# Attention rows replicated through one transpose and DRAM, loads spread over 16 blocks, later output stores, a tanh ring of ten, a new order of work

## The chip, the cores and the metric

The kernel runs on one core of a Trainium2 chip. The metric is the device time of one execution in microseconds. A profile is one further execution; its span is some 2 us shorter than the time taken for it. As there is one core, a run is called slow here only when it is more than 1.5% above the fastest of the same kernel. The kernel before was timed in every session beside what it is compared with; its medians in the five sessions were 735.8 to 738.6 us.

## The reference, cut to what matters

```python
B, N, m, C = (4, 12416, 32, 128)
def mab(q, kv):                         # attention of q over kv
    s = scale * (q @ kv.transpose(0, 2, 1)); s = s - s.max(-1, keepdims=True)
    a = np.exp(s); a /= a.sum(-1, keepdims=True) + 1e-09
    return a @ kv
h = mab(I, x)                           # 32 inducing rows attend to all 12416 tokens of a batch
x = mab(x, h)                           # every token attends to those 32 rows
gate = 1.0 / (1.0 + np.exp(-(x @ w_gate)))          # then a gated feed-forward layer, 128 -> 1536 -> 128
out = (gate * (x @ w_val)) @ w_out
```

The h of a batch needs all of its x. So the next batch is loaded, transposed and reduced to h while the present batch is in the feed-forward layer.

## The kernel before: the parts that matter

Tokens go through in 97 blocks of 512, 24 blocks a batch and one mixed block of tails. In each block PE makes gate and value columns (the fills, one helper line), ScalarE takes the tanh of the gates into a ring of T tiles, VectorE multiplies (1 + T) by the value out of PSUM, and PE multiplies by w_out. A string, PLAN, fixes the order of these within each block; the letter J in it takes the next of the extra jobs (scores, h, and so on) of the next batch. In 23 of the blocks ScalarE copies three of the twelve value columns to SBUF, and GpSimd multiplies them.

```python
tp = ctx.enter_context(tc.tile_pool(name="tp", bufs=8))          # the tanh ring
def load_x(b, q):            # 512 KB of fp16, cast on the way: issued by GpSimd
    nc.gpsimd.dma_start(t[:], x[b, ds(q * QT, QT)].rearrange("(p j) c -> p (j c)", j=QT // P))
def xT_dma(b, q):            # transposed for the scores: issued by SyncE
    nc.sync.dma_start(xTs[b][...], xqs[(b, q)][:], transpose=True)
# attention weights of 2048 tokens: normalize, repeat for four row groups, transpose 512 KB
for r in range(4):
    nc.gpsimd.tensor_tensor(out=a2[:, r], in0=e2n[...].to_broadcast(...), in1=rc[...].to_broadcast(...), op=ALU.mult)
nc.sync.dma_start(rep[:, 4 * i:4 * i + 4]..., a2[:]..., transpose=True)
# value columns that GpSimd takes; reads the tanh tile
nc.gpsimd.tensor_tensor(out=t[:], in0=v, in1=Ts[(bi, j0 // 2)][:, j0 % 2 + jj, :], op=ALU.mult)
nc.gpsimd.tensor_tensor(out=u[:, jj, :], in0=t[:], in1=v, op=ALU.add)
# ... cut: prologue, h, output; output transposes are issued by SyncE, output stores by GpSimd
```

The softmax here doesn't subtract the row's maximum and nothing guards it: scores larger than these inputs give would overflow.

Of the kernel before, what the change touches and what calls it, by code (L numbers as in the profile page):

```python
# [22 lines left out]


PLAN = (
    "GAGBWGAabGBcGAfeGBdGAhBWgJ AGilkjBGGAabcBGfAGBedWAGhBGg AGilBkjAGJBabAGcfBWeAGdBgGh "
    "AGilkBjGAGBabcGAefGBdGAhgBGi AGlBJkAGjBWAGBbacfGAedGBghG AikljBJGAaWBbcGAfeGBdGAhBGgG "
    "AilGBkjAGBWabGAceBGfGAdhgiBG AGlkBjJAGBbGacAGfeBGdG AgBJhAGilBkjGAGbaBceAGfdGBgG "
    "AhiGBlGAkjJBGAGbaBGcGAeBJf AGdhBGgAGiBlkjGAGBabef AGcdGBhGAgiBkljGAGBabceAGfBJdG "
    "AhgiBGAGlkjBJGABbWacfGAeBdGgh AGikGBlGAjJBGAGbacBfeGAGdhBgG AikGBlGAjJBGAGabBGcGAfeBGd "  # L30
    "AGhgiBGAGlkjBJGABaGbfG AeGcBdGAhgBWiJkljAGBGabcGAfedBgG AGhiBlGAJkBjAGGBabcGAfGBedG "
    "AhJBgGAikljBGGAabfBecG AGBdghGAilkjBGGAbaBcfGAGBedG AhGBgiGAlkjBGGAbacBGfAGBedGh "
    "AGgBiGAGklBjGAGBbacfAGedBGh AGgBGiAGkljBGGAabBcefGAGdhBgG AilkjBGGAbaBceGAGfdBhG "
    "AgGBikGAljBWGAabcBeGAGfdBhG AgGBikGAljBGGAbaGBcGAefGBdG AhBJgAGilkBjGAGbBaeG "
    "AfcGBdGAghBGiGAlkjBGAGbacBfG AeGBdhGAgiWBlGAkjBJGAbacBfeG AGdBghiGAlkjBJGAaGbBcGAfGeBdG "
    "AhGgBiGAlGkBjGAGBbacfAGedBGg AGhiBGlAGkjBJAGBGbaeG AfGcBdGAgJBhGAikljBGGAabcBfeG "
    "AdghBiGGAlkBjJAGBabcGGAfeBGdG AgBJhAGilkBjGAGaBbfe AGdcGBgGAhikBljGAGBabceAGfBJdG "
    "AhgBGiAGlkjBJGABbGaceGAfdWBhg AGiGBklGAjJBGAGbaBcWAGfeBdG AhGBgiGAlGBkGAjJBGAGbGBacG "
    "AfeGBdGAhgBGiGAlkjBJG AabGBfeAGdGBhgGAciBWlJkjAGBGbacG AfBJeAGdhGBgGAikljBGGAbBJa "
    "AGceBGfAGdBhGgAGiBlkjG AGBabefAGdgBGhcAGilkjBGGAabcBeG AfGdBhGAgGBilGAkjBWGAabBcGe "  # L40
    "AGfBGdAGgBhWAGiBlkjAGGBbace AGfdBGhAGgilBkjAGGBbacGAeGfBdG AhGBgiGAlkjBWGAabBefdG "
    "AGcBhgGAilkjBGGAabcBeGAfGdBhG AgGBiGAlkjBGGAbaBcGGAfeBdG AGhBGgAGilBkjAGJBba "
    "AGfeBGdAGcBhgGAGilkBjGAGBbace AGfBJdAGhgiBGAGkljBWAGBbacfeG AdGBhgGAikljBJGAaWBbcGAefGBdG "
    "AghGBiGAlBGkjAGBWbaAGcfBGe AGdgBhiGAGklBjJAGBGabf AGeBJdGAchBGgAGiklBjGAGaBbce "
    "AGfdGBgGAhiGBkGAljJBGAGbaBGcG AfBJeAGdgBGhAGilkBjG AGBabefAGdgBGhGAcikBljGAJbBac "
    "AGefBGdGAhgBiGAGlkjBJGABWbacfG AGeBdhgAGikGBlGAjJBGAGabBcefG AGdhBgGAilGBkGAjJBGAGabBGcG "
    "AfeBGdAGhgBGiAGlkjBJG ABabGfeAGdBhGgGAciBWlJkjAGBGabcG AeBJfAGdhGBgGAiklBjGGAbaBcfG "
    "AGeBdhgGAilkjBGAJeBfG AbWBadGAhgGBcGAilkjBGGAbacBfG AeGBdGAgGhBiGAlkjBGGAabBcGf "
    "AGedBGhAGgBiGAGlkBjGAGBbacf AGedBGhAGgBGiAGkljBGGAabcBefG AdgGBhGAilkjBGGAbaBfeG "
    "AdGBcgGAhGBilGAkjBWGAabcBfG AGedBgGAhGBilGAkjBGGAbBJa AGcfBGeAGdgBGhAGilkBjG "  # L50
    "AGBbafeAGdgGBhGAcikBljGAGBabce AGfdGBhGAgikBljGAGBbacfAGedgGBhG "
    "AikljBGGAabcBGAfWBedGAhgGBiG AlkjBJGAbGBacGAfeBGdGAhGBgiG AlkjBGGAbafBeGAdWBhgG "
    "AcGBilGAkjGBGAabBceGAfGdBG AhGgBiGAkljBGGAbaBcfGAGBJe AGdhBGgAGiklBjGAGBefba "
    "AGdhGBgGAickBljGAGBbaceAGfdBWgG AhikBljGAGBbacGAfeBGdGAhgiGBG AkljBGGAbacBGAfWBedGAhGBgiG "
    "AlkjBGGAbacBGAGfeBGAGdhBgiG AGkBljGAGBbafAGeBdgG AGhcBiGAGkBljGAGBabcAGfBeGd "
    "AGgBGhAGilBkjGAGBbacGAfGBedG AhgGBiGAlkBjGGAbBafeG AdGBchGAgGBilGAkjBWGAbacBefG "
    "AGBdghGAilBkjGGAbaBcfGAedGBhG AgiGBlGAkjBWGAabBceGAfGdBhG AgGiBkGAljBGGAbacBeGAGfdBhgiG "
    "AlkjBGGAabBefcGAdhBgGG AiklBjGABabcAfedBAghBilkj"
)
SHARED = (2, 7, 10, 15, 18, 23)  # L60


@with_exitstack
def kernel(
# [28 lines left out]
    ep = ctx.enter_context(tc.tile_pool(name="ep", bufs=2))  # L93
    ap_ = ctx.enter_context(tc.tile_pool(name="ap", bufs=2))
    repp = ctx.enter_context(tc.tile_pool(name="repp", bufs=2))
    tp = ctx.enter_context(tc.tile_pool(name="tp", bufs=8))
    up = ctx.enter_context(tc.tile_pool(name="up", bufs=5))
    vp = ctx.enter_context(tc.tile_pool(name="vp", bufs=1))
    outp = ctx.enter_context(tc.tile_pool(name="outp", bufs=3))
    smp = ctx.enter_context(tc.tile_pool(name="smp", bufs=2))  # L100

# [263 lines left out]

    def a2_mul(b, d, i):
        e2n, rc = e2s[(b, d)], e2s[(b, d, "rc")]
        a2 = ap_.tile([P, 4, 4, 4, M], F16, tag="a2", name=f"a2_{b}_{d}_{i}")
        for r in range(4):
            nc.gpsimd.tensor_tensor(  # L370
                out=a2[:, r], in0=e2n[:, i, :, r, :].unsqueeze(2).to_broadcast((P, 4, 4, M)),
                in1=rc[:, i, :, r].unsqueeze(2).unsqueeze(3).to_broadcast((P, 4, 4, M)),
                op=ALU.mult,
            )
        e2s[(b, d, i, "a2")] = a2

    def rep_tile(b, d):
# [1 line left out]
            reps[(b, d)] = repp.tile([P, 8, 4, P], F16, tag="rep", name=f"rep_{b}_{d}")  # L379
        return reps[(b, d)]  # L380

    def rep_dma(b, d, i):
        rep = rep_tile(b, d)
        a2 = e2s.pop((b, d, i, "a2"))
        nc.sync.dma_start(
            rep[:, 4 * i:4 * i + 4].rearrange("p r j t -> p (r j) t"),
            a2[:].rearrange("p r j g m -> p (r j g m)"), transpose=True,
        )


    blocks = []
# [276 lines left out]

    BB = 8 * ND
    ev = {}  # L670
    extra = {}

    def at(n, k, fn, *a):
        ev.setdefault((n, k), []).append(lambda: fn(*a))

    def put(n, *a):
        assert n not in extra
        extra[n] = a

    def rep_events(n, b, d):  # L680
        put(n, "s2", b, d)
        at(n + 1, 1, e2_dma, b, d)
        at(n + 1, 3, s2_sum, b, d)
        at(n + 2, 3, s2_rec, b, d)
        at(n + 2, 3, a2_mul, b, d, 0)
        at(n + 3, 1, rep_dma, b, d, 0)
        at(n + 3, 1, a2_mul, b, d, 1)
        at(n + 4, 0, rep_dma, b, d, 1)

    def m_mul():  # L690
        e2s["m", "a2"] = s2n_mul("m", 0, nc.gpsimd, B)
# [11 lines left out]
    def q1_dma(r):  # L703
        rep_blk(e2s["q1", r], 4 + r)

    put(0, "s2q")
    at(1, 0, s2n_sum, "q1", 0, 16)
    for r in range(4):
        at(1, r, q1_mul, r)
# [3 lines left out]
    for b in range(B):  # L713
        n0 = b * BB
        rep_events(n0 + 2, b, 1)
        rep_events(n0 + 10, b, 2)
        nb = b + 1
        if nb < B:
            plan = (
                ((1, 0), (2, 0), (2, 2), (3, 2), 4, (5, 2), (7, 9)),  # L720
                ((5, 0), (6, 0), (6, 2), (7, 2), 8, (9, 2), (12, 13)),
                ((8, 0), (9, 0), (9, 3), (10, 2), 11, (12, 2), (14, 15)),
            )
            for e, (l0, l1, x0, x1, s1, a1, hs) in enumerate(plan):
                qs = [2 * e, 2 * e + 1]
                for q, lo, xo, h in zip(qs, (l0, l1), (x0, x1), hs):
                    at(n0 + lo[0], lo[1], load_x, nb, q)
                    at(n0 + xo[0], xo[1], xT_dma, nb, q)
                    put(n0 + h, "h", nb, q)
                if e == 0:  # L730
                    at(n0 + l1[0], l1[1], load_tail, nb)
                    at(n0 + x1[0], x1[1], xTt_dma, nb)
                put(n0 + s1, "s1", nb, qs)
                at(n0 + a1[0], a1[1], a1_dma, nb, qs)
            put(n0 + 5, "s1t", nb)
            put(n0 + 16, "hfin", nb)
            put(n0 + 17, "hw", nb)
            at(n0 + 18, 1, hw_pad, nb)
            rep_events(n0 + 18, nb, 0)
        else:  # L740
            put(n0 + 6, "s2m")
            at(n0 + 7, 1, s2n_sum, "m", 0, B)
            at(n0 + 7, 1, m_mul)
            at(n0 + 8, 1, m_dma)
# [36 lines left out]
            s2n_exp("m", ps, 0, B)  # L781
        return None

    jobs = deque((n, extra[n]) for n in sorted(extra))

    def chunks(k):

# [33 lines left out]
    def out_one(n, j):  # L821
        out_mm(n, j, us.pop((n, j)))
        if done_out[n] == NJ:
            out_store(n)
        if stores and (done_out[n] == NJ // 2 or n >= NBK - 2):
            stores.popleft()()

    words = PLAN.split()
# [2 lines left out]
    for n, word in enumerate(words):  # L831
        steps = [k for k in range(4) if not (n in shared and k == 0)]
        si = -1
        for c in word:
            if c == "A":
                si += 1
                for k in range(steps[si - 1] + 1 if si else 0, steps[si] + 1):
                    for f in ev.get((n, k), ()):
                        f()
                ps = slot_a(f"va_{n}_{steps[si]}")  # L840
                j = chunks(steps[si])[0]
                v_fill(ps, n, j, 2)
                v_mul(ps, n, j, 2)
            elif c == "B":
                ps = slot_b(f"vb_{n}_{steps[si]}")
                j = chunks(steps[si])[1]
                v_fill(ps, n, j, 1)
                v_mul(ps, n, j, 1)
            elif c in "GW":
                next_slot(c == "W")  # L850
            elif c == "J":
                post = do_extra(*jobs.popleft()[1])
                if post:
                    post()
            else:
                out_one(cur, ord(c) - ord("a"))
                if done_out[cur] == NJ:
                    cur += 1
# [33 lines left out]
```

## Time and profile before

| | before |
|---|---|
| median of its runs beside the first of the change | 738.2 us (736.6 to 745.5) |
| span of the profile | 739.5 us |
| first VectorE product of block 0 | 29.9 us |
| VectorE idle after 30 us | 43.0 us |
| the same from 30 to 130 us (prologue's end and most of batch 0) | 13.0 us |
| the same from 130 to 600 us | 29.7 us |
| ScalarE idle, waiting for GpSimd to read a tanh tile | 16.0 us |

The span is VectorE's busy time and its idle time, and the busy time hardly changes (669.4 us before, 666.2 after), so idle time of VectorE is most of what a change can win. I use it as the account in all that follows; the 2 to 4 us that it misses are named at the end. These two stretches of the profile before give rows four and five (length, then busy PE, PEld, DVE, ACT, POOL, granted clock, DMA share, GB/s):

```profile
30.00:130.00 100.00, 89.35 (x568) 28.79 (x567) 87.03 (x101) 87.47 (x101) 45.08 (x55) 0.95 0.84 138
130.00:600.00 470.00, 445.64 (x2776) 146.52 (x2773) 440.29 (x519) 435.42 (x503) 253.72 (x298) 0.97 0.56 108
```

### The profile page before, as it was taken

What the parts mean: (1) busy time and instruction counts of PE and PEld (TensorE: products, weight loads), DVE (VectorE), ACT (ScalarE), POOL (GpSimd) and SP (SyncE); (2) the same over time, 40 slices, a digit from 0 to 9 for tenths busy, and PEclk for the clock granted to TensorE, in tenths of its full rate; (3) what the DMA queues carried; (4) which work ended last, traced back from release to release, by engine and by line L of the source; (5) the groups of instructions that cost most, each with busy time, mean ns of one, the idle gap of its engine ahead of it and who ended that gap; (6) DMA issues with size and microseconds to landing.
All of it is one profiled execution on the core that took longest, in us unless ns stands there. A gap on an engine that the chain in (4) does not pass through costs nothing.

```text
span 739.5 us, 12973 instructions
## 1 busy us (share of the span) xinstructions
PE 690.5 (93%) x4561; PEld 237.6 (32%) x4561; DVE 669.4 (91%) x792; ACT 664.6 (90%) x773; POOL 377.7 (51%) x455
## 2 busy tenths in 40 slices
PE   7898979999989979999999896999999999999996
PEld 4432323333322323333333221333333333333334
DVE  2698969999979969999999794999999999999996
ACT  4798969999989969999999785999999999999994
POOL 5234624636635655464575273464664565654432
PEclk9999989999999989999999898999999999999999
DMA  9594987523529598652356789743334253262223
GB/s 177 85 147 96 190 146 147 122 58 80 105 46 159 114 201 142 117 118 48 79 121 118 114 155 157 151 109 87 77 82 92 63 115 89 65 114 66 62 52 73
DMA packets 181906, 80.17 MB, mean 108 GB/s; under 512 B 165424, under 2 KB 166096, under 8 KB 181840
## 3 DMA queue, kind: packets, MB, share of 16 engines
q1 hardware_dynamic: 161856, 40.18, 31.9%
q0 software_dynamic: 19696, 39.03, 24.8%
q8 instruction: 35, 0.57, 0.3%
q14 instruction: 31, 0.25, 0.1%
q10 hardware_dynamic: 288, 0.13, 0.1%
HBM read 27.80 MB, written 25.43 MB: 72 GB/s over the span
## 4 chain that ended last, share of the span: by engine, by line
PE 56%; DVE 17%; DMA 8%; ACT 7%; issue 5%; POOL 4%; SPq 3%; ACTq 0%; POOLq 0%; DVEq 0%
DMA xq_4_130<-in_x_dram 2%; SPq L192 2%; DMA xT_154<-xq_3_6108 1%; DMA xT_153<-xq_3_3697 1%; DMA xT_154<-xq_1_5713 1%; DMA xq_1_5713<-in_x_dram 1%; DMA xT_152<-xq_1_873 1%; DMA xT_152<-xq_3_1295 1%; PE acc_1451 L526 0%; PE acc_6516 L526 0%; PE acc_5235 L526 0%; PE acc_8733 L526 0%; PE acc_5888 L526 0%; PE acc_8829 L526 0%; PE acc_7267 L526 0%
## 5 line engine op out<-in xcount | busy, mean ns | idle before, releaser
L526 PEld LDWEIGHTS <-wo_115 128*128 128x128 f16 x1152 | 94.9, 98 | 151.6 <-issue 99.1
L416 PEld LDWEIGHTS <-hw_163 32*128 32x128 f16 x462 | 19.1, 91 | 60.2 <-issue 57.9
L416 PEld LDWEIGHTS <-hw_164 32*128 32x128 f16 x466 | 19.4, 91 | 59.3 <-issue 57.0
L416 PEld LDWEIGHTS <-hw_166 32*128 32x128 f16 x466 | 19.9, 91 | 55.9 <-issue 53.8
L416 PEld LDWEIGHTS <-hw_165 32*128 32x128 f16 x466 | 19.1, 91 | 57.5 <-issue 55.2
L416 PEld LDWEIGHTS <-hwp_167 128*128 128x128 f16 x114 | 10.9, 98 | 16.8 <-issue 9.9
L416 PEld LDWEIGHTS <-hwp_170 128*128 128x128 f16 x110 | 10.6, 97 | 15.2 <-issue 7.8
L416 PEld LDWEIGHTS <-hwp_168 128*128 128x128 f16 x110 | 10.7, 98 | 14.0 <-issue 7.0
L416 PEld LDWEIGHTS <-hwp_169 128*128 128x128 f16 x110 | 10.6, 99 | 13.7 <-issue 6.9
L244 PEld LDWEIGHTS <-ones 128*128 128x128 f16 x96 | 7.0, 97 | 4.5 <-issue 2.1
L751 PEld LDWEIGHTS <-indT 128*32 128x32 f16 x72 | 1.6, 95 | 21.4 <-issue 16.9
L189 PE MATMUL warm<-ones 128*128 128x512 f16 x16 | 6.0, 561 | 1.5 <-DVE ones L139 1.5
L483 DVE SCALAR_TENSOR_TENSOR u_4_6338<-T_2_6286,va_1_6335 128x1024 f16<-128x1024 f16 x1 | 1.2, 1221 | 6.8 <-PE va_1_6335 L416 6.8
L309 POOL COPY hwp_167<-hw_163 32x128 f16<-32x128 f16 x2 | 0.6, 284 | 13.1 <-ACT hw_163 L302 13.0
L370 POOL TENSOR_TENSOR a_1_0_0_2814<-e2n_0_2665,rc_0_2812 128x512 f16<-128x512 f16 x4 | 4.1, 1040 | 6.0 <-DVE rc_0_2812 L360 6.0
L370 POOL TENSOR_TENSOR a_0_2_0_1993<-e2n_2_1813,rc_2_1991 128x512 f16<-128x512 f16 x4 | 4.1, 1038 | 5.8 <-DVE rc_2_1991 L360 5.8
L370 POOL TENSOR_TENSOR a_0_1_0_1154<-e2n_1_1000,rc_1_1152 128x512 f16<-128x512 f16 x4 | 4.1, 1049 | 5.4 <-DMA on_1117<-oT_1115 5.4
L213 ACT ACTIVATE e_3_2_6327<-s_3_6318 128x1024 f16<-128x1024 f32 x1 | 1.0, 1024 | 6.3 <-PE s_3_6318 L751 6.3
L370 POOL TENSOR_TENSOR a_2_1_0_5971<-e2n_1_5810,rc_1_5969 128x512 f16<-128x512 f16 x4 | 4.1, 1039 | 5.0 <-DVE rc_1_5969 L360 5.0
L751 PE MATMUL s_3_6318<-xT_154,indT 128*32 128x512 f16 x8 | 1.0, 495 | 5.9 <-DMA xT_154<-xq_3_6108 4.6
L483 DVE SCALAR_TENSOR_TENSOR u_4_1515<-T_2_1445,va_1_1512 128x1024 f16<-128x1024 f16 x1 | 1.2, 1221 | 5.7 <-PE g_1_1517 L416 5.7
L370 POOL TENSOR_TENSOR a_2_0_0_5225<-e2n_0_5066,rc_0_5223 128x512 f16<-128x512 f16 x4 | 4.1, 1039 | 4.2 <-DVE rc_0_5223 L360 4.2
(4281 smaller groups left out, 2864.2 us busy)
## 6 DMA issues: line engine op xcount, KB each, us to landing
xq_0_118<-in_x_dram POOLq DMA_DIRECT2D x1, 512.0 KB, 5.2
xq_1_120<-in_x_dram POOLq DMA_DIRECT2D x1, 512.0 KB, 7.3
xq_2_126<-in_x_dram POOLq DMA_DIRECT2D x1, 512.0 KB, 8.6
xq_3_128<-in_x_dram POOLq DMA_DIRECT2D x1, 512.0 KB, 10.6
xq_4_130<-in_x_dram POOLq DMA_DIRECT2D x1, 512.0 KB, 14.0
xq_5_132<-in_x_dram POOLq DMA_DIRECT2D x2, 256.0 KB, 14.7
xq_0_768<-in_x_dram POOLq DMA_DIRECT2D x1, 512.0 KB, 6.3
xq_1_873<-in_x_dram POOLq DMA_DIRECT2D x1, 512.0 KB, 6.1
```

Source lines behind the costliest of these rows:

```text
L189: nc.tensor.matmul(ps[:, 0:TOK], ones[:, 0:P], ones[:], start=True, stop=True)
L192: nc.sync.dma_start(xTs[b][:, ds(q * QT, QT)].rearrange("c (j p) -> c j p", p=P), xqs[(b, q)][:], transpose=True,)
L213: nc.scalar.activation(out=e1[:, 0:w], in_=ps[:, 0:w], func=AF.Exp, scale=SCALE)
L244: nc.tensor.matmul(ps[:, cs:cs + P], ones[:, 0:P], a1n[(b, q)][:, j, :], start=first and j == 0, stop=last and j == 3,)
L309: nc.gpsimd.tensor_copy(out=pads[b][rows, 2 * i + jj, :], in_=hws[b][rows, p, :])
L370: nc.gpsimd.tensor_tensor(out=a2[:, r], in0=e2n[:, i, :, r, :].unsqueeze(2).to_broadcast((P, 4, 4, M)), in1=rc[:, i, :, r].unsqueeze(2).un ...
L416: nc.tensor.matmul(ps[:, ds(col, TOK)], weights(k["b"]), rep[rows, 4 * k["i"] + k["r"]], start=True, stop=True,)
L483: nc.vector.scalar_tensor_tensor(out=u[:, :, 0:T], in0=Ts[(bi, j0 // 2)][:, j0 % 2:j0 % 2 + n, 0:T], scalar=1.0, in1=ps[:].rearrange("p (a ...
L526: nc.tensor.matmul(accs[bi][:, 0:T], wo16[:, j, :], u, start=(c == 0), stop=(c == NJ - 1))
L751: nc.tensor.matmul(ps[r * M:(r + 1) * M, ts(i, TOK)], indT[:], xTs[a[0]][:, ds(q * QT + r * TOK, TOK)], start=True, stop=True,)
```

## The change

Its intent: less work for GpSimd and fewer transposed bytes per half of attention rows; the loads of batches 2 and 3 not in pairs just before their use, but one by one, over 16 blocks; output stores issued later, when the transposed output is more likely to have landed; more room between ScalarE and the readers of its tanh tiles. PLAN is new throughout, and so are the blocks in which GpSimd takes columns (SHARED).

```diff
-    tp = ctx.enter_context(tc.tile_pool(name="tp", bufs=8))
+    tp = ctx.enter_context(tc.tile_pool(name="tp", bufs=10))
+    dp = ctx.enter_context(tc.tile_pool(name="dp", bufs=2, space=bass.MemoryType.DRAM))
-        a2 = ap_.tile([P, 4, 4, 4, M], F16, tag="a2", ...)
-        for r in range(4):
-            nc.gpsimd.tensor_tensor(out=a2[:, r], ...)
+        a2 = ap_.tile([P, 4, 4, M], F16, tag="a2", ...)
+        nc.gpsimd.tensor_tensor(out=a2[:], in0=e2n[:, i], in1=rc[:, i]..., op=ALU.mult)
-        nc.sync.dma_start(rep[:, 4 * i:4 * i + 4]..., a2[:]..., transpose=True)
+        nc.sync.dma_start(a2T[:], a2[:]..., transpose=True)          # a2_dma
+        nc.sync.dma_start(dt[:], a2T[:]...)                          # rep_put: to DRAM
+        for g in range(4):                                           # rep_get: back, four times
+            nc.sync.dma_start(rep[g * M:(g + 1) * M, 4 * i:4 * i + 4]..., dt[:]...)
...  loads of a batch, by block from the start of the batch before it:
-                ((1, 0), (2, 0), ...), ((5, 0), (6, 0), ...), ((8, 0), (9, 0), ...)
+            if b == 0:
+                loads = ((1, 0), (2, 0), (5, 0), (6, 0), (8, 0), (9, 0))
+                s1s, s1t, fin = (5, 9, 12), 6, 16                    # scores one block later
+            else:
+                loads = ((-10, 0), (-7, 0), (-4, 0), (-1, 0), (2, 0), (5, 0))
+                s1s, s1t, fin = (-2, 5, 9), 0, 14
...
-        if stores and (done_out[n] == NJ // 2 or n >= NBK - 2):
+        if stores and (done_out[n] == 10 or n >= NBK - 2):
-SHARED = (2, 7, 10, 15, 18, 23)
+SHARED = (3, 7, 11, 15, 19, 23)
```

## The prediction

> **What bounds the kernel now**
>
> I read the page first, then the busy time by stretch, then the waits of VectorE, then the chain of waits inside one bad stretch, then the DMA issues of SyncE. The page says that three engines are nearly full:
>
> ```profile
> PE 690.5 (93%) x4561; PEld 237.6 (32%) x4561; DVE 669.4 (91%) x792; ACT 664.6 (90%) x773; POOL 377.7 (51%) x455
> ```
>
> An average cannot say whether the missing 9% of DVE is spread evenly or sits in a few holes, so I cut the span into stretches of 10 us and then joined them into good and bad stages. Columns: length, busy time of PE, PEld, DVE, ACT, POOL, then granted clock, DMA share, GB/s.
>
> ```profile
> 60.00:130.00 70.00, 60.85 (x398) 19.34 (x394) 58.05 (x68) 57.96 (x68) 34.65 (x42) 0.93 0.82 140
> 130.00:200.00 70.00, 68.85 (x440) 23.14 (x438) 69.05 (x85) 67.26 (x78) 40.35 (x48) 1.00 0.39 84
> 200.00:280.00 80.00, 70.47 (x409) 22.33 (x408) 68.11 (x78) 68.20 (x80) 41.66 (x47) 0.94 0.76 135
> 280.00:395.00 115.00, 114.56 (x746) 38.60 (x742) 114.49 (x137) 113.04 (x131) 63.50 (x76) 1.00 0.50 100
> 395.00:470.00 75.00, 62.70 (x374) 19.56 (x372) 58.94 (x69) 58.64 (x70) 35.59 (x42) 0.91 0.84 142
> 470.00:600.00 130.00, 129.07 (x817) 42.89 (x815) 129.70 (x154) 128.28 (x148) 72.60 (x87) 1.00 0.43 92
> ```
>
> In good stages DVE is busy 114.49 of 115 and 129.70 of 130 us: VectorE is the bound there, with ScalarE 1 to 2 us behind it. All else is in three bad stages, which are the first halves of batches 0, 1 and 2, where the next batch is loaded: DVE idles 11.95, 11.89 and 16.06 us, 39.9 us in all, and the DMA share is 0.76 to 0.84. The waits of VectorE name the holes (who, for what, us, times, longest):
>
> ```profile
> DVE u_4_6338 L483 <- PE va_1_6335 L416: 6.8, 1, 6.8
> DVE u_4_1515 L483 <- PE g_1_1517 L416: 5.7, 1, 5.7
> DVE u_4_3803 L483 <- ACT T_5_3797 L470: 5.5, 1, 5.5
> ...
> DVE u_4_5924 L483 <- PE g_5_5926 L416: 4.2, 1, 4.2
> DVE u_9_3036 L483 <- PE vb_3_3034 L416: 2.9, 1, 2.9
> ...
> DVE u_8_6247 L483 <- PE vb_2_6245 L416: 2.5, 1, 2.5
> ```
>
> Behind these are two causes. The chain of waits at 440 us (start, length, what) shows the first: the score matmuls of the next batch (L751) sit in PE's order, and their transposed x is not there yet.
>
> ```profile
> 440.98 6.01 SPq L192
> ...
> 447.06 8.48 DMA xT_154<-xq_3_6108
> ...
> 455.58 0.62 PE s_3_6318 L751 x4
> ```
>
> The second is GpSimd. ScalarE's waits hold T_3_3766 <- vt_1_3714 for 5.1 us: a tanh tile cannot be overwritten before GpSimd has read the old one for its share of the products, and GpSimd was late, as it issues the output stores in order and sat before them:
>
> ```profile
> POOL out_dram L554 <- DMA on_3837<-oT_3835: 9.5, 1, 9.5
> POOL out_dram L554 <- DMA on_6252<-oT_6250: 9.5, 1, 9.5
> ```
>
> Both come from the transposing DMAs queued together on SyncE. From 252 to 282 us eight of them (three of 128 KB, one of 256, four of 512) are in its queue, with three loads of 512 KB issued beside them. A 128 KB output transpose lands in 2.4 us at the median and needed 7.7 us there; an x transpose took 4.3 at best and 8.5 there. By first causes: late x transposes 6.8 + 5.7 + 4.2 + 2.0 = 18.7 us, the late GpSimd 5.5 + 2.9 + 2.5 + 1.1 = 12.0, and 9.2 us of small waits, many just after a hole, while the clock is still down (0.68 in 450 to 460 us).
>
> [...]
>
> [...] 2.4 us became 7.7 beside loads. [...]
>
> [...]
>
> [...] 10 us windows with holes have granted clocks of 0.68 to 0.83, the good stages 1.00. So removing a hole also removes its slow exit.
>
> [...] The hot DVE instruction reads one SBUF and one PSUM tensor, and I averaged its durations: 1217 ns beside busy GpSimd, 1220 ns beside an idle one. So a lighter GpSimd makes no DVE instruction shorter.
>
> **The change part by part**
>
> 1. Replication. Before, each of 22 half-pairs cost GpSimd four multiplications of 1.04 us and SyncE one transpose of 512 KB (landing 4.7 us at the median, 11.0 at worst). After: one multiplication, one transpose of 128 KB (2.4 us, from the output transposes of that size), one 128 KB write to DRAM and four reads of 128 KB. GpSimd loses 66 x 1.04 = 69 us of 378, none on the path directly. Transposed volume falls by 22 x 384 KB. SyncE's issue time, per pair of halves: two transposes of 1.2 us plus ten plain DMAs at 0.4 us (the two plain loads at the start) = 6.4 us against some 3; over 11 pairs about 37 us more, on a queue that spends 278 of 739 us issuing.
>  The chain for a first half: before 4.1 (multiplications) + 4.7 = 8.8 us. After: 1.0 + 2.4 + 2.1 (write; the last output stores, plain and from SyncE, took 1.7 and 2.2) + 1.2 (three issues ahead of the last) + 2 = 8.7. As an estimate, equal.
>  Is there room? I walked both instruction orders and counted only VectorE's time between events (1.22 and 0.68 us an instruction). From the get of the first half to the first matmul that needs it there were 13.3 to 17.2 us; now 7.6 to 10.7 (24.7 for first pairs of batches 2 and 3). The four reads need perhaps 3.5 us. Enough.
>
> 2. Loads. By the same walk, the time from the issue place of an x transpose to its score matmul was 5.7 and 5.7 us in batch 0, 9.5 and 7.3 in batch 1, 5.7 and 6.1 in batch 2 at the bad pairs; all four holes of cause one are at places of 5.7 to 6.1, and the 7.3 one was late too (landed 278.7, used at 278.8). Places with 10 us or more show no hole. After, the least is 11.4 (batch 0, last pair); the next is 14.5, and batches 1 and 2 have 21 to 57. Worth 18.7 us plus the slow exits. From exponent transpose to its h matmuls the least falls from 13.3 to 9.5 us against a 3.4 us landing: no new hole.
>
> 3. Stores. A store is issued after the tenth instead of the sixth output matmul of the next block: 4/12 of a 7.2 us block = 2.4 us later, so GpSimd waits less at its head.
>
> 4. Tanh ring of ten instead of eight: two tiles of 1.02 us more before ScalarE meets an unread tile. With 2, 3 and the lighter GpSimd this takes away most of the 12.0 us.
>
> 5. The plan itself: same count of G, A, B and extra jobs, 34 instead of 30 widened fills on PE. DVE work is unchanged.
>
> Sum: first product at 29.9 us; DVE busy after 30 us 661.2; from DVE's last end to the end 5.2. Floor 30 + 661.2 + 5.2 = 696.4 in the profiled span. The good stages idle 0.5 of 115 and 0.3 of 130, so 700 us at that rate add about 2: 698.5. I leave 3 to 4 us for batch 0, whose loads stay near the start, where the DMA share is 1.16 to 1.25 in several windows, and for small new waits of the round trip: **702 us**. In terms of the median that is 738.8 - 37, of the 39.9 in the bad stages.
>
> **Rivals**
>
> A. The round trip blocks SyncE. Its waits stand ahead of output and x transposes, rep arrives late, and PE waits for it at each eight-block border. For: three DMAs in series, least room 7.6 us. Against: the chain is no longer than before, and the puts and gets are placed half a block apart. If each of 11 pairs lost 2 us: 724.
>
> B. ScalarE or PE takes over as the bound. For: ACT is 650 of 702 us in the stages, 9 us below DVE. Against: in good stages DVE is above 99.5% although both are as full. It would cost 2 to 4 us: 705.
>
> C. The load holes were only half of it: batch 0 keeps its load places, and only the use moves one block later. If batch 0 keeps 8 of its 12 us: 710.
>
> D. Transfers were hidden, the holes only move: nothing gained, 735. Against: the stages without loads have no holes, with the same GpSimd and SyncE work per pair.
>
> **Range and chances**
>
> 702 with 695 to 713: the lower end is the floor, the upper holds C and a mild A. The 2% line is at 724, which takes a full A or D. Faster 0.9, same 0.08, slower 0.02.
>
> **What would show it**
>
> Right: stages of 60 to 130, and those at the start of batches 1 and 2, with DVE at 98% or more and clock 1.00; no wait of L751 on xT over 1 us; no T waiting on vt over 1 us; GpSimd near 309 us busy; DVE still about 669. Wrong: fills (L416) that wait for rep tiles, SyncE standing before puts or gets while an x transpose is due, or DVE idle over 20 us after the first 30.

## The result, and the profile after

The changed kernel took 712.2 us in the median of four runs: 715.1, 712.5, 702.8 and 712.0. Before: 738.2. The ratio is 0.9587, 95% interval 0.9467 to 0.9708. Ratios here are the mean time of one kernel's fast runs over that of the other's of the same rounds, so they are not quite the ratio of the medians quoted beside them. The prediction was 702 with a range of 695 to 713. So the direction and the range held, and the gain was 26 us where 37 was predicted.

The four runs are not alike: the one of 702.8 us had a mean granted clock of 0.999, the others 0.990 to 0.992. The profiled execution is the longest of the four and counts as slow, 1.7% above the fastest. The unedited kernel was therefore profiled once more (first experiment); what I conclude below is in both profiles or says so. Its page says, for the line of busy times that the prediction shows of before:

```profile
PE 679.8 (95%) x4561; PEld 238.2 (33%) x4561; DVE 666.2 (93%) x792; ACT 662.5 (93%) x773; POOL 309.6 (43%) x389
```

GpSimd lost 68 us, as worked out. VectorE's durations add up to 717.2 us in both kernels; the 3 us less of busy time are overlap of neighbouring instructions. The stages that were bad before, in the changed kernel:

```profile
60.00:130.00 70.00, 59.98 (x364) 18.83 (x363) 55.85 (x66) 55.29 (x65) 27.86 (x33) 0.90 1.13 148
...
200.00:280.00 80.00, 77.42 (x525) 26.00 (x524) 78.00 (x92) 78.06 (x92) 34.32 (x39) 1.00 0.77 145
...
395.00:470.00 75.00, 72.97 (x515) 25.08 (x515) 73.42 (x87) 71.93 (x84) 37.06 (x44) 1.00 0.60 122
```

Batches 1 and 2 are mended: VectorE idles 2.0 and 1.6 us there, where it idled 11.9 and 16.1, and the clock is 1.00. Batch 0 isn't: 14.2 us idle where there were 12.0, at a clock of 0.90 and a DMA share of 1.13 instead of 0.82. The blocks come earlier in the changed kernel, so the same stretch holds a little other work. Over wider stretches it is the same picture:

```profile
30.00:130.00 100.00, 88.83 (x535) 28.16 (x535) 84.72 (x100) 84.42 (x98) 36.66 (x45) 0.93 1.06 141
130.00:600.00 470.00, 460.77 (x2944) 155.82 (x2942) 464.39 (x550) 459.53 (x535) 216.95 (x266) 1.00 0.64 125
```

Idle is 15.3 and 5.6 us, against 13.0 and 29.7 before. The clock is 0.70 from 80 to 90 us and 0.76 from 110 to 120, with and just after the holes of batch 0, and 1.00 after 120 us. A run with a clock of 0.999, such as that of 702.8 us, can hardly have had these holes. ScalarE's waits for GpSimd's reads fell from 16.0 us to 0.3. What is left are two holes, by VectorE's waits:

```profile
DVE u_8_1670 L495 <- PE vb_2_1668 L428: 6.4, 1, 6.4
DVE u_4_1402 L495 <- PE va_1_1399 L428: 4.2, 1, 4.2
```

and what PE waited for in them:

```profile
PE s_1_1657 L767 <- DMA xT_154<-xq_2_1174: 4.2, 1, 4.2
PE g_0_1394 L428 <- DMA rep_1_1278<-dt_1_0_1230: 3.6, 2, 2.4
```

The smaller hole, at block 8, is a wait of the new kind: the first fill of the second group of eight blocks wants a rep tile that is still on its way back from DRAM. The larger is of the old kind: scores without their transposed x. SyncE's DMA issues in that time (start, length, what) show how they come about:

```profile
68.96 3.16 SPq L562 DMA_TRANSPOSE on_1197<-oT_1195  x1
72.21 1.37 SPq L384 DMA_TRANSPOSE a2T_1_1_1204<-a_0_1_1_1149  x1
73.68 0.53 SPq L390 DMA_DIRECT2D dt_1_0_1230<-a2T_1_0_1172  x1
80.22 0.33 SPq L390 DMA_DIRECT2D dt_1_1_1254<-a2T_1_1_1204  x1
80.64 1.89 SPq L397 DMA_DIRECT2D rep_1_1278<-dt_1_0_1230  x4
...
87.24 5.78 SPq L193 DMA_TRANSPOSE xT_154<-xq_2_1174  x1
```

The second put waits from 74.2 to 80.2 for its transpose to land, and the gets of the first half stand behind it. The x transpose stands behind them all and goes out at 87.24, 9.6 us after its place in the program (the VectorE product that follows it there began at 77.6 us). GpSimd issues an x load at 87.50. PE was ready for the scores at 104.2 us, but the transpose landed at 108.3. The times to landing (last figure) of that stretch, issued between 66 and 112 us:

```profile
xq_4_1469<-in_x_dram POOLq DMA_DIRECT2D x1, 512.0 KB, 18.5
...
a2T_1_1_1204<-a_0_1_1_1149 SPq DMA_TRANSPOSE x1, 8.0
...
xT_154<-xq_2_1174 SPq DMA_TRANSPOSE x1, 21.1
on_1411<-oT_1409 SPq DMA_TRANSPOSE x1, 15.7
xT_154<-xq_3_1283 SPq DMA_TRANSPOSE x1, 13.2
```

Of the twelve x loads and the twelve x transposes from 130 us on, the loads took 6.3 us at the median (5.7 to 8.7) and the transposes 5.0 (4.2 to 5.8). Here a load took 18.5, a transpose 21.1.

### The profile page after: what moved, and what is told of

Read it like the earlier page. It is cut to its first block, busy times and chain, and to the rows that moved or that the text cites. A ratio compares the mean times of both kernels' runs of the same rounds, so it can differ in the third digit from the quotient of the medians.

```text
span 713.3 us, 13070 instructions
## 1 busy us (share of the span) xinstructions
PE 679.8 (95%) x4561; PEld 238.2 (33%) x4561; DVE 666.2 (93%) x792; ACT 662.5 (93%) x773; POOL 309.6 (43%) x389
## 4 chain that ended last, share of the span: by engine, by line
PE 64%; ACT 10%; DVE 9%; DMA 8%; issue 4%; POOL 3%; SPq 1%; DVEq 0%; ACTq 0%; POOLq 0%
DMA xq_4_132<-in_x_dram 2%; DMA xT_154<-xq_3_1283 2%; DMA a2T_1_1_1204<-a_0_1_1_1149 1%; SPq L397 1%; DMA a1n_2_3819<-e_2_2_3703 1%; DMA on_7763<-oT_7761 1%; DMA a1n_2_6256<-e_3_2_6162 1%; DMA on_5277<-oT_5275 1%; PE acc_1687 L538 1%; DMA rep_1_1278<-dt_1_0_1230 0%; PE acc_4267 L538 0%; PE acc_2641 L538 0%; PE acc_1770 L538 0%; PE acc_5765 L538 0%; PE acc_3334 L538 0%
## 5 line engine op out<-in xcount | busy, mean ns | idle before, releaser
L428 PEld LDWEIGHTS <-hwp_172 128*128 128x128 f16 x120 | 11.7, 97 | 14.3 <-issue 4.7
## 6 DMA issues: line engine op xcount, KB each, us to landing
xq_1_875<-in_x_dram POOLq DMA_DIRECT2D x1, 512.0 KB, 10.1
```

The source lines that it names most:

```text
L428: nc.tensor.matmul(ps[:, ds(col, TOK)], weights(k["b"]), rep[rows, 4 * k["i"] + k["r"]], start=True, stop=True,)
```

## The experiments

Twelve kernels ran, all of them correct. Each was timed in at least one round, most in three. "DVE idle" is read from each profile as above, first from 30 to 130, then from 130 to 600 us.

| run | median us (range) | ratio to before, 95% | DVE idle, us |
|---|---|---|---|
| before | 738.2 (736.6 to 745.5) | 1 | 13.0, 29.7 |
| changed | 712.2 (702.8 to 715.1) | 0.9587 (0.9467 to 0.9708) | 15.3, 5.6 |
| after_again | 710.2 (706.6 to 716.9) | 0.9602 (0.9547 to 0.9657) | 15.6, 6.9 |
| ring8 | 720.1 (712.6 to 724.0) | 0.9718 (0.9647 to 0.9789) | 6.3, 17.6 |
| old_rep8 | 714.4 (711.9 to 715.2) | 0.9669 (0.9630 to 0.9709) | 8.4, 9.2 |
| late_loads | 727.6 (722.8 to 740.5) | 0.9832 (0.9778 to 0.9887) | 8.1, 24.1 |
| rep_alone | 738.1 (733.1 to 740.2) | 0.9999 (0.9942 to 1.0056) | 12.5, 26.2 |
| pro3 | 704.8 (701.8 to 706.3) | 0.9553 (0.9506 to 0.9600) | 2.7, 4.9 |
| old_rep8_pro3 | 711.3 (708.8 to 711.9) | 0.9640 (0.9595 to 0.9684) | 4.4, 10.8 |
| store6 | 708.7 (706.8 to 711.1) | 0.9606 (0.9550 to 0.9660) | 10.1, 5.3 |
| q4_late | 710.6 (704.0 to 711.4) | 0.9609 (0.9555 to 0.9663) | 3.3, 6.0 |
| pro3_ring8 | 713.5 (710.9 to 714.9) | 0.9646 (0.9597 to 0.9695) | 3.4, 12.7 |
| pro3_store6 | 702.8 (701.7 to 708.6) | 0.9521 (0.9463 to 0.9579) | 6.0, 7.5 |
| q4_late_b | 704.3 (700.4, 708.3) | 0.9581 (0.9443 to 0.9718) | 2.6, 3.9 |

The median and range are of all runs, the ratio of fast ones alone; one run of ring8 (724.0) and one of late_loads (740.5) count as slow. Three sessions, on different chips, hold after_again to late_loads; rep_alone, pro3, old_rep8_pro3 and store6; q4_late, pro3_ring8 and pro3_store6. Across them only the ratios to before are compared. A profile is of one execution: of the longest run in changed, after_again and pro3_store6, of the fastest in pro3, q4_late and q4_late_b. So the last column shows what can happen in a kernel, and not its mean.

Theory at the outset: the gain is the spread loads of batches 1 and 2, and what fell short is batch 0, whose load places stayed. Rivals: the lighter replication did it; the ring or the stores did it; batch 0's hole was a rare bad moment.

### after_again: the changed kernel, no edit

> The changed kernel again, unedited, for a second profile and its spread. Theory A (the remaining 12 to 14 us of VectorE idle in batch 0 are made by the order of transfers in SyncE's queue, so they come back every time): median near 711, holes again between 60 and 130 us, DVE idle there over 8 us. Theory B (the 21 us x transpose of the first profile was a rare slow moment of the DMA engines): most runs near 703, and the same stage idles under 5 us.

The holes came back: 15.6 us of idle before 130 us, one hole of 11.5 us at 112 us, and in it the same pair of transfers, issued 0.4 us apart, took 22.7 (transpose) and 21.9 us (load). So it is no freak. But this is again the profile of the longest run, and the times of the single runs lie between 706.6 and 716.9, so it doesn't strike every run alike. That the order in SyncE's queue makes the holes, as theory A says, is not shown by this. The hole at block 8 cost PE just 0.5 us of waiting in this profile.

### late_loads: the loads of batches 2 and 3 in pairs again

```diff
-                loads = ((-10, 0), (-7, 0), (-4, 0), (-1, 0), (2, 0), (5, 0))
+                loads = ((-5, 0), (-4, 0), (2, 0), (3, 0), (6, 0), (7, 0))
```

> Changed kernel, but the loads of batches 2 and 3 are issued in pairs three to four blocks before their scores, jobs in the same places. If spreading them was worth the 24 us that the bad stages of batches 1 and 2 lost less: 15 to 25 us slower, near 730, with scores waiting for xT in both batches. If the lighter transposes were what mattered: under 6 us slower.

0.9832 over 0.9602 is 1.024: 17 us slower than the changed kernel, on the same chip and in the same rounds. Idle after 130 us rises from 6.9 to 24.1 us, and PE waits for transposed x again (third figure: the longest):

```profile
PE s L767 <- DMA xT<-xq: 14.1, 5, 5.8
```

Nothing but the places of the loads, and of the transposes tied to them, differs; the pairs stand three and two blocks before their scores, as in the kernel before. So in the changed kernel spreading them is worth about 17 us, the largest part that any single run here shows.

### ring8: the changed kernel with a ring of eight

```diff
-    tp = ctx.enter_context(tc.tile_pool(name="tp", bufs=10))
+    tp = ctx.enter_context(tc.tile_pool(name="tp", bufs=8))
```

> Changed kernel with the tanh ring back at eight. If the longer ring carried its share of the 12 us of late-GpSimd holes by itself: 3 to 8 us slower than the changed kernel. If the lighter GpSimd and later stores already removed them: within 2 us of it, and no T tile waits over 1 us for a vt product.

0.9718 over 0.9602 is 1.012: nearly 9 us slower; the two intervals just touch. ScalarE again waits for GpSimd to read its tiles (total, times, longest), although GpSimd has 68 us less to do than before and stores are issued late:

```profile
ACT T L482 <- POOL vt L508: 8.9, 10, 1.4
```

So the two tiles more take away these last 8.9 us; the other parts of the change don't. They may have had a share in the fall from 16.0 to 8.9.

### old_rep8: the changed kernel with the old replication, ring of eight

```diff
-        nc.gpsimd.tensor_tensor(out=a2[:], in0=e2n[:, i], ...)
+        for r in range(4):
+            nc.gpsimd.tensor_tensor(out=a2[:, r], ...)
-        # a2_dma, rep_put, rep_get at blocks n+3 and n+4
+        # rep_dma at (n+3, 1) and (n+4, 0), one 512 KB transpose each
```

A first build kept the ring of ten and did not fit: 4.78 KB a partition were left where the last pool needed 8. That is a result too. The old a2 tiles take 2 x 4 KB a partition, the new a2 and a2T together 2 x (1 + 1) KB, and a tanh tile is 2 KB: the new replication frees just the two tiles that the ring got.

> Changed kernel with the replication of before (four multiplications, one 512 KB transpose, no DRAM trip), ring eight because ten does not fit beside it. Compare with ring8. Theory A1 (the new replication is what frees the DMA queue and GpSimd): 8 to 20 us slower than ring8, T tiles waiting for vt and 4 us more GpSimd work per half. Theory A2 (spreading the loads did nearly all): within 4 us of ring8; if the round trip is what makes batch 0 late, even 3 to 8 us faster there.

Beside ring8 (0.9718) it came out at 0.9669, so the old replication was if anything faster; the two intervals overlap. Here too ScalarE waits for GpSimd, no longer than in ring8, with 67 us more GpSimd work (376.2 against 309.5):

```profile
ACT T L471 <- POOL vt L497: 7.5, 9, 1.4
```

Theory A1 is out. PE also waited 4.2 us at block 8 for its rep tile: with these load places that hole does not need the round trip.

### rep_alone: the kernel before with the new replication alone

```diff
-        # four multiplications, one 512 KB transpose
+        # one multiplication, one 128 KB transpose, a put and four gets, at the places of the change
```

> The kernel before with the new replication alone (one multiplication, small transpose, DRAM trip), all else as before. Theory A1 (lighter transposes and GpSimd were worth the 12 us of late-GpSimd holes): 6 to 14 us faster than before. Theory A2 (after old_rep8 came out 5.7 us faster than ring8: the round trip itself gains nothing and holds SyncE up): within 4 us of before, or slower by up to 8, with fills waiting for rep tiles.

The ratio is 0.9999. Idle is 12.5 and 26.2 us against 13.0 and 29.7, and ScalarE waits 8.4 us for GpSimd, where it waited 16.0: the lighter GpSimd may halve these waits, but no time comes of it. By itself this part of the change is worth nothing, with an interval of 0.6% either way.

### store6: the changed kernel with stores at the old place

```diff
-        if stores and (done_out[n] == 10 or n >= NBK - 2):
+        if stores and (done_out[n] == NJ // 2 or n >= NBK - 2):
```

> Changed kernel with the output stores issued after the sixth output matmul again. If issuing them later was worth something by itself (GpSimd no longer stands before a store while the transposed output is under way): 3 to 8 us slower than the changed kernel, GpSimd waiting longer for on tiles and T waiting for vt. If the ring of ten covers it: within 2 us of 710.

0.9606 against 0.9602: no difference. In its profile the first hole of batch 0 was there (PE waited 4.4 us for a rep tile), the second was absent (0.8 us in blocks 8 to 15): in GpSimd's order the loads moved too, and none was issued within a microsecond of an x transpose.

### pro3: batch 0's loads spread as well

```diff
+    for q in range(3):               # at the end of the prologue
+        load_x(1, q)
-                loads = ((1, 0), (2, 0), (5, 0), (6, 0), (8, 0), (9, 0))
+                loads = (None, None, None, (3, 0), (7, 0), (9, 0))
+                xs = ((1, 2), (2, 2), (3, 2), (4, 0), (8, 2), (10, 2))    # x transposes
```

> Changed kernel with batch 0's loads spread: three of the next batch's six loads are issued in the prologue, where the DMA share is 0.2 at 30 to 40 us, and the other three at blocks 3, 7 and 9. Theory C (the crowd of loads, transposes and rep transfers at 40 to 120 us in batch 0 makes the remaining 16 us of holes): idle of the first 16 blocks under 6 us, median 699 to 704, and no x transpose over 12 us. If the holes came from the round trip's order in SyncE's queue and not from the crowd: still 10 us or more of them, about 710.

Both holes are gone from the profile. Its span is 700.0 us, and its stretches are these:

```profile
30.00:130.00 100.00, 96.88 (x641) 32.24 (x640) 97.30 (x116) 96.80 (x113) 39.80 (x50) 1.00 0.85 143
130.00:600.00 470.00, 461.24 (x2911) 155.90 (x2907) 465.15 (x549) 460.21 (x536) 213.82 (x260) 1.00 0.62 123
```

Batch 0 idles 2.7 us instead of 15.3, at a DMA share of 0.85 instead of 1.06, with the same round trips through DRAM and the same SyncE order of puts and gets. The median is 704.8. Its four runs lie within 4.5 us, those of the two sessions of the changed kernel within 14. The profile supports theory C, that the crowd of transfers made batch 0's holes, and speaks against the order of the queue alone. But it is of pro3's fastest run (701.8 us, clock 0.999; the others took 704.4 to 706.3 at 0.994 to 0.996), beside the longest of the changed kernel, so 12.6 us less idle is not what the spreading is worth on the average. The ratio is 0.5% below that of the changed kernel in other rounds, with overlapping intervals, so the 5 to 7 us are what the medians say, not a settled size.

### old_rep8_pro3 and pro3_ring8: the two replications in the uncrowded kernel

> The same spread loads with the replication of before and a ring of eight. Theory C with A2: 702 to 708, the first hole (rep late at block 8, 4.5 us) gone, T tiles still waiting for vt about 7 us in all, as in old_rep8. If the 512 KB transposes fill the queue: no better than old_rep8, 714.

> The spread loads of pro3 with a ring of eight, to compare with old_rep8_pro3 (711.3) and pro3 (704.8). If the two tiles more are what the new replication pays for and the replication itself is neutral: 709 to 713, T waiting for vt 7 to 9 us in all. If the lighter GpSimd helps by itself once the crowd is gone: 705 to 708. If the round trip still costs: over 714.

Their edits are those above, combined. 0.9640 and 0.9646: with the same ring and the crowd gone, the replications are alike to 0.1%, and 67 us of GpSimd work between them are worth nothing. pro3 with its ring of ten is at 0.9553, so the two tiles are worth 1% again, 7 us; here too the intervals just touch, so it is the two settings together that show it. The expectation that old_rep8_pro3 might reach 702 was too low.

### pro3_store6

> The spread loads of pro3 with stores after the sixth output matmul. store6 was 708.7 against 710 to 712 for the changed kernel, but it also moved the loads apart in GpSimd's order. If the store place is worth nothing by itself: within 2 us of pro3. If late stores help GpSimd: 3 us or more slower.

0.9521 against 0.9553 of pro3; the intervals overlap. Late stores are not worth anything in either setting. This is the lowest median of all, 702.8, but its profile was its longest run, so I don't call it better than pro3.

### q4_late and q4_late_b: one load moved away from one transpose

```diff
-                loads = ((1, 0), (2, 0), (5, 0), (6, 0), (8, 0), (9, 0))
+                loads = ((1, 0), (2, 0), (5, 0), (6, 0), (8, 3), (9, 0))
```

> Changed kernel with one load moved: the fifth load of batch 0 three quarters of a block later, so that it comes after the next output store and is not issued within 0.5 us of the x transpose of the third piece (21.1 and 22.7 us to land in the two profiles). If that meeting makes the second hole of batch 0 (6.4 and 11.5 us): the third piece's transpose lands in under 10 us, DVE idle in blocks 8 to 15 under 2 us, median 702 to 707; the first hole, at block 8, may stay. If the slow transfers have another cause: hole and median as before, 710.

In the profile it did what was expected: the third piece's transpose landed in 5.9 us instead of 21, idle in blocks 8 to 15 was 0.8 us, and that execution took 704.0 us. SyncE was as late as before: the transpose went out at 86.1 us. So lateness alone doesn't make the hole. The x transposes from 80 to 112 us in after_again, then in q4_late:

```profile
DMA to landing us min/median/max: 11.2/15.1/22.7
...
DMA to landing us min/median/max: 4.6/5.5/6.7
```

But the four other runs took 709.1 to 711.4. So the median did not move, and the second half of the expectation failed. A second look was to show such a run:

> The kernel q4_late again: its profiled execution was its best (704.0), the four others took 709.1 to 711.4. A second profile is to show where such a run loses 6 us. If the first hole (fills that wait for the first rep tile at block 8, 4.2 us and its slow exit) comes and goes with the timing: a run near 710 with 8 us or more of DVE idle in the first eight blocks and under 2 us in the second eight. If a load still meets an x transpose in those runs: an x transpose over 11 us and a hole in the second eight.

It did not: the profiled run took 700.4 us with 0.8 us in blocks 8 to 15 and 2.7 in blocks 0 to 7, and the other run 708.3. What a run of 710 us of this kernel loses stays open, as no profile caught one. The granted clocks say a little: 0.988 to 0.991 in the five slower runs, 0.994 and 1.000 in the two profiled ones. As the clock of the profiles was low with and after holes (0.70 and 0.76 in 10 us windows of the changed kernel), the slower runs most likely had holes too; where is not known.

All 14 profiles together hold 252 x transposes. Set out by the time between their issue and that of the nearest x load still under way beside them:

| issued apart | transposes | us to landing: least, median, most |
|---|---|---|
| no load beside it | 170 | 4.2, 5.1, 8.0 |
| over 2.1 us | 56 | 4.2, 5.7, 15.1 |
| 0.7 to 2.1 us | 16 | 6.8, 8.5, 10.1 |
| up to 0.4 us | 10 | 11.1, 11.7, 22.7 |

The two over 11 us in the second row are those queued behind the 21.1 and 22.7 us ones. A transpose issued within 0.4 us of a load was held up in all ten cases, and in the two slowest the load was too, with 18.5 and 21.9 us; beside a transpose of 11.1 us in the changed profile the load took 7.3. The medians of 6.3 and 5.0 us above add up to 11.3, so as a rough estimate 11 to 14 us is what the two would take one after the other, but that they go one after the other is not shown. In ring8 and late_loads the same transpose met its load, landed in 11.6 and 13.9 us, and made PE wait for no scores there. The 21.1 and 22.7 us are more than that: over the 21.1 us all queues together moved about 90 GB/s, where the stage as a whole made 148. Why they took twice as long is not shown.

## Why the prediction came out as it did

**The bound was right.** It is VectorE, with three bad stages. The floor of 696 to 698.5 us was about 4 us too high: it took VectorE's 661.2 us after 30 us as fixed, but in all profiles with a ring of ten they are 657 to 658. The durations add up to the same; neighbours overlap more, and why is not shown. By the same sum pro3's span of 700.0 us is a floor of 692.3 and 7.7 us of idle. On the other side the 702 us are a sum of the profiled span, and a run's time is 1.8 us longer. That these two slips partly cancel is luck.

**The loads (step 2) were right for batches 1 and 2**: the walk said 21 to 57 us of room, and no wait of scores for x is left there. late_loads puts their worth at 17 us.

**The step that failed is the remainder for batch 0**, "I leave 3 to 4 us for batch 0". In the two profiles of the changed kernel it kept all of its hole: 15.3 and 15.6 us of idle before 130 us, where 13.0 had been. All three of the prediction's signs of being wrong are in the first of them: 21.0 us of idle after the first 30, fills that waited 3.6 us for a rep tile, and SyncE standing before puts while an x transpose was due. Both profiles are of the longest run, and the run of 702.8 us hit the prediction without these holes, by its clock; so the holes cost some runs much and others little. The medians, 712.2 and 710.2, are 10 and 8 us above 702, and pro3 takes 5 to 7 us off.

What was mis-sized is the time to landing. Redone, the walk gives the pair that made the hole, the second, 22.1 us for its first transpose and 16.4 for its second; the tightest, with 11.4, is the third, and it made no wait. In the trace these 22 us shrank to 17, as the transpose went out late, and then it took 21.1 instead of the 4.3 to 8.5 that the prediction had seen. Rival C, with 710 for a batch 0 that keeps 8 of 12 us, was the nearest; I should have trusted the DMA share of 1.16 to 1.25, which I quoted, more than the places.

**The equal chain of step 1 was right on average.** rep_alone at 0.9999, and 0.9640 beside 0.9646, say that the round trip is neither gain nor loss. In batch 0 rep came 3.6 us late in one profile and 0.5 in another, but 4.2 us late in old_rep8, which has no round trip; so this is not shown to be rival A.

**Steps 3 and 4 were credited to the wrong parts.** I gave the late-GpSimd holes to loads, stores and the lighter GpSimd together with the ring. Without the ring 6.7 and 8.9 us of ScalarE's waits are left, and the ring is worth 9 us in one setting and 7 in the other; the later stores and the 67 us less of GpSimd work show no gain. Not all of the ring's gain is idle time: VectorE's busy time is 665.8 to 666.8 us in the profiles with ten tiles and 668.5 to 669.6 in those with eight. I also missed what the new replication is for: it pays for the ring, as its smaller tiles free 4 KB a partition.

Loads 17 and ring 9 make 26 us, the measured gain, but each was measured by taking it alone out of the changed kernel, and that they add up is not shown. The new PLAN, SHARED and the later scores were never run with the old loads and the old ring, so a share of theirs is not ruled out.

**One reading** of the prediction was too neat. The windows with holes have clocks of 0.68 to 0.89 (0.89 from 200 to 210 us), not just up to 0.83, and it did not take a long hole: a gap of 1.9 us in PE's work, at 61 to 63 us, was followed by a slower clock (0.83 from 60 to 70 us).

## What to carry to other kernels

Take work off an engine only where something waits for its result: 68 us less on GpSimd changed nothing that could be measured, while two more buffers between it and ScalarE were worth 7 to 9 us, and the worth of a leaner step may be the memory that it frees for such buffers. Where a stage is late because transfers crowd, look at when each is really issued, behind what its queue waits for, and not at its place in the program (an x transpose of the changed kernel went out 9.6 us after it); then move transfers to where the DMA share is low (from 30 to 130 us pro3's profile had a share of 0.85 instead of 1.06, and 2.7 us of idle instead of 15.3). Read the stage that the change leaves as it is with the same distrust as those that it mends.

## What the transfers cost, as measured

- A 512 KB transpose and a 512 KB casting load issued within 0.4 us of each other: 11.1 to 22.7 us until the transpose landed (10 cases), against a median of 5.1 with no load beside it (170 cases). The results were correct in all runs.
- A transpose from SBUF to SBUF landed, at best, in 2.4 us for 128 KB and in 4.3 us for 512 KB, in the kernel before. As a rough estimate from these two, which differ in shape too, the 384 KB more took 1.9 us more, or 207 GB/s.
- The 167 transposes of the changed profile held SyncE, which issues them, for 1.19 us at least and 1.21 at the median; the least was 1.19 us for those of 128 KB and 1.34 for the x transposes of 512 KB. The longest held it for 11.1 us, at 97.4 us, while two earlier transposes were still under way; in after_again the longest x transpose between 80 and 112 us held it for 13.0. The 114 plain DMAs that SyncE issued in the changed profile held it 0.43 us at the median, and 0.32 to 2.15 us in all.
